# Queries of twelve of twenty-four groups loaded as eight-token runs and put in order by four copies out of PSUM

## The chip, the cores and the metric

The kernel runs on one core of one Trainium2 chip. The time is the device time of one execution in microseconds (us); the kernel before took 178.64 us as the median of three runs (177.48 to 182.0). Another execution was recorded by the hardware profiler; durations below come from that one.

The core has an engine for matrix products (PE; its weight loads are PEld), three engines for elementwise work (DVE, ACT, POOL), and SP, which here only issues DMAs. Sixteen DMA engines move the data. SBUF and PSUM are the on-chip memories, both with 128 partitions; matrix products land in PSUM.

## The reference

Four batches, eight heads, 768 tokens, head dimension 64, all fp32. A linear attention with a per-head decay `lam` comes first, then a layer that changes 128 chosen tokens of each batch:

```python
# attention, blocks of 64 tokens
intra = (q @ k.T * Dmask) @ v             # inside the block
inter = (q * lam_pow) @ kv_state          # from the blocks before
kv_state = lam_block * kv_state + (k * rev_pow).T @ v
# x: the heads side by side, 512 values for each token
scores = x @ w_gate
top    = the 128 highest scores of each batch
out[top] = x[top] + sigmoid(scores[top]) * (relu(x[top] @ w1) @ w2)
```

## The kernel before

A **group** is 128 tokens of one batch with all eight heads; there are 24 groups, numbered 0 to 23, six for each batch. For every group `load(g)` (L66 to L83) issues three DMAs from SP's queue: keys (`kn`), queries (`qn`) and values (`vn`), 256 KB each. In all three a partition holds one token: its row is eight pieces of 64 values, one for each head. In DRAM these pieces lie 768 tokens apart, so a piece, and a packet of the DMA, is 256 bytes, and a load has 1,024 packets.

`transposes(g, name)` (L192) turns the queries and the keys so that the head dimension lies over the partitions. For each pair of heads PE transposes a 128x128 block into a quarter of a PSUM bank (L203), and one ACT copy takes the whole bank into SBUF (L207). So `qT` has the two heads of a pair on partitions 0 to 63 and 64 to 127, and for each of the four pairs 128 tokens in order. POOL multiplies `qT` by the powers of the decay (`qs`, L216); PE reads `qT` for the scores (L240) and `qs` for the part from the states (L340).

The order of the work is written out by hand. The loop at L682 runs over g. For g of 11 and more (the second branch, L753) one pass is, on PE: the transposes of group g+1, queries first; one piece of the expert layer; `from_states(g)` (L340); `state_products(g+1)` (L287); the sums and the row for the ranking (L472, L434); two more pieces (L564 or L576); `from_scores(g)` (L363); `scores(g+1)` (L240). ACT follows in the same order: the copies of `qT` and `kT` (L207), then what the pieces and the ranking leave in PSUM (L540, L568, L437), then the three copies that make `x_b` (L391, L393). POOL runs `qs`, the decayed state (L300) and the decayed keys (L185). PSUM has four banks `m` that are handed out in turn.

SP takes its DMAs in order. At the start of pass g, `loads_to(g + ahead(g), g)` issues the loads of groups up to g + 4 (rising to 8 ahead), and after them some of the weights of the expert layer (`w_sb`, L97 and L102). At the end of the pass comes the store of finished groups (L398). The second branch first transposes group 12 in pass 11. Each group has its own buffers out of eight, and a DMA waits for the one eight before it on SP's queue.

Of the kernel before, what the change touches and what calls it, by code (L numbers as in the profile page):

```python
# [17 lines left out]
def kernel(  # L18
# [12 lines left out]
    nc = tc.nc  # L31
# [5 lines left out]
    L = 128  # L37
# [11 lines left out]
    WEIGHTS = {8: 1, 9: 2, 10: 1, 11: 3, 12: 3, 13: 2}  # L49
    WIDE = 11  # L50
    WARM = 8
    TINY = 2.0 ** -125
    BELOW = TINY * (1.0 - 2.0 ** -24)

# [7 lines left out]

    half = [slice(0, C), slice(C, 2 * C)]
    loaded = {}

    def load(g):  # L66
        b, c = divmod(g, NT)
        rows = slice(c * L, (c + 1) * L)
        srcs = (("kn", k), ("qn", q), ("vn", v))
        tiles = [ld.tile([128, H, D], FP32, name=name) for name, _ in srcs]  # L70
        whole, front, back = slice(0, H), slice(0, H // 2), slice(H // 2, H)
        order = [(x, whole) for x in range(3)]
        if g == 0:
            order = [(0, front), (1, front), (0, back), (1, back), (2, whole)]
        for x, hs in order:
            if (g, x) == (2, 2):
                nc.sync.dma_start(
                    out=wg_b[:], in_=moe_w_gate.unsqueeze(0).broadcast_to([128, HD])
                )
            nc.sync.dma_start(  # L80
                out=tiles[x][:, hs], in_=srcs[x][1][b, hs, rows, :].rearrange("h p d -> p h d")
            )
        loaded[g] = tiles  # L83
# [3 lines left out]
    wg_b = const.tile([128, HD], FP32, name="wg_b")  # L87
    wg_o = const.tile([128, HD], FP32, name="wg_o")
    load(0)
    load(1)  # L90
    load(2)
    w1_sb = const.tile([128, NDC, F], FP32, name="w1_sb")
    w2_sb = const.tile([128, NFC, HD], FP32, name="w2_sb")
# [18 lines left out]
    for hp in range(NHP):  # L112
        for hh in range(2):
            h = 2 * hp + hh
            nc.vector.tensor_tensor_scan(
                out=mask_w[:, hh, hp, :], data0=lam_b[:, h : h + 1].broadcast_to([128, L]),
# [35 lines left out]
    def warm(n):  # L152
        for _ in range(n):
            nc.tensor.matmul(
                free[-1][:, :L], lhsT=zero[:], rhs=zero[:], start=True, stop=True,
                skip_group_check=True,
            )

    warm(WARM)

    def bank(hold=False):
        t = next(t for t in free if not any(t is x for x in held))
        free[:] = [x for x in free if x is not t] + [t]
        if hold:
            held.append(t)
        return t

    qTs, qss, kTs, kds, ps_ = {}, {}, {}, {}, {}
# [23 lines left out]
    def transposes(g, name, part=None):  # L192
        if g >= NG:
            return
        t = loaded[g][1 if name == "qT" else 0]
        dsts = qTs if name == "qT" else kTs
        hps = range(NHP) if part is None else range(part * NHP // 2, (part + 1) * NHP // 2)
        if not part:
            banks_[name] = bank()
            dsts[g] = att.tile([128, NHP, L], FP32, name=name)  # L200
        tp = banks_[name]
        for hp in hps:
            nc.tensor.transpose(  # L203
                tp[:, hp * L : (hp + 1) * L], in_=t[:, 2 * hp : 2 * hp + 2, :], identity=ident[:]
            )
        at = slice(hps[0] * L, (hps[-1] + 1) * L)
        nc.scalar.copy(out=dsts[g][:].rearrange("p a i -> p (a i)")[:, at], in_=tp[:, at])  # L207

# [415 lines left out]
    def constants():  # L624
        nc.gpsimd.memset(lead[:], TINY)
        nc.gpsimd.affine_select(
            out=lead[:], in_=lead[:], compare_op=ALU.is_ge, fill=-BELOW,
            base=0, pattern=[[1, L]], channel_multiplier=-1,
        )
        nc.gpsimd.memset(ones[:], 1.0)  # L630
        nc.gpsimd.iota(slot_i[:], pattern=[[1, 128]], base=0, channel_multiplier=0)
        nc.gpsimd.iota(place_i[:, 0], pattern=[[1, NG]], base=0, channel_multiplier=0)
        nc.gpsimd.iota(place_i[:, 1], pattern=[[0, NG]], base=0, channel_multiplier=1)
# [48 lines left out]
    for g in range(-1, NG):  # L682
# [3 lines left out]
        if wide(g):  # L686
# [7 lines left out]
            if g < 0:  # L694
                for part in range(2):
                    transposes(0, "kT", part)
                    transposes(0, "qT", part)
# [4 lines left out]
            elif g == 0:  # L702
                transposes(1, "kT")
                from_scores(0, 0)
                transposes(1, "qT")
                from_scores(0, 1)
                outputs(0)
                store(0)
                queries_decayed(1)
                nc.scalar.copy(  # L710
                    out=decay_w[:], in_=qpow[:, :, L - 1 : L].broadcast_to([128, NHP, D])
                )
                decay_state(2)
            else:
                for name in ("kT", "qT") if g == 1 else ("qT", "kT"):
                    transposes(g + 1, name)
                queries_decayed(g + 1)
                from_scores(g)
                if g == 1:
                    nc.scalar.copy(  # L720
                        out=wg_o[:].rearrange("p (a b e) -> p a b e", a=2, e=D),
                        in_=wg_b[:].rearrange("p (b a e) -> p a b e", a=2, e=D),
                    )
                    gate_scores(0)
                outputs(g)
                store(g)
                gate_scores(g)
# [113 lines left out]
```

## Time and profile before

| what | value |
|---|---|
| time, median of 3 runs | 178.64 us (177.48 to 182.0) |
| time of the profiled execution | 179.35 us |
| its span | 177.6 us |
| PE busy | 161.5 us (91%) |
| DVE, ACT, POOL busy | 99.1, 68.9, 86.2 us |
| packets of the DMA queues | 82,608, of which 75,792 under 512 bytes |
| bytes moved | 32.20 MB |
| load of queries, 256 KB, issue to landing (median) | 5.1 us |
| TensorE clock, mean | 0.994 |

The span is what the profiler recorded from the first to the last instruction; the time of that execution is 1.75 us longer, and the execution is 0.71 us above the median of the three runs. The profile has the busy time of each engine, the same in 40 slices of the span, the DMA queues, a chain of waits followed back from the last instruction, the costliest groups of instructions, and the DMA issues. The trace behind it can be asked for windows of time and for single instructions, and holds a record of every DMA packet with its size and duration.

### The profile page before, as it was taken

How to read it: one execution, taken by the hardware profiler on the slowest of the kernel's cores; microseconds unless marked ns; L12 is line 12 of the kernel's file. 1: busy time of each engine (PE TensorE's matmuls, PEld its weight loads, DVE VectorE, ACT ScalarE, POOL GpSimd, SP SyncE). 2: the span in 40 equal slices, each digit the busy share in tenths (PEclk: the TensorE clock that was granted, in tenths of full speed). 3: DMA queues.
4: the chain of work that ended last, by engine and by line, in shares of the span. 5: the costliest groups of instructions: out<-in, count | busy, mean ns of one | idle time of the engine just before them, and what ended most of it. 6: DMA issues, size and time to landing. Idle time of an engine off the chain costs nothing.

```text
span 177.6 us, 7490 instructions
## 1 busy us (share of the span) xinstructions
PE 161.5 (91%) x3228; PEld 133.7 (75%) x3228; DVE 99.1 (56%) x304; ACT 68.9 (39%) x173; POOL 86.2 (49%) x96
## 2 busy tenths in 40 slices
PE   7998988999998999899695989999998999999990
PEld 7687966789887989897363679887665699559970
DVE  2876957678694748635627457647565767030011
ACT  3344436453343545434332364556244353013100
POOL 1396562546667656547374755827756300202022
PEclk9999999999999999999999999999999999999997
DMA  4999989999989999988989999999412131201000
GB/s 108 223 223 206 238 196 224 234 233 252 209 187 266 285 251 243 325 217 284 265 286 241 230 251 212 207 231 232 147 63 80 44 122 59 63 0 59 0 30 30
DMA packets 82608, 32.20 MB, mean 181 GB/s; under 512 B 75792, under 2 KB 77840, under 8 KB 82576
## 3 DMA queue, kind: packets, MB, share of 16 engines
q1 hardware_dynamic: 81776, 29.63, 70.3%
q0 software_dynamic: 656, 2.10, 3.9%
q8 instruction: 25, 0.41, 1.0%
q14 instruction: 7, 0.06, 0.1%
q10 hardware_dynamic: 144, 0.00, 0.0%
HBM read 24.38 MB, written 7.34 MB: 179 GB/s over the span
## 4 chain that ended last, share of the span: by engine, by line
PE 61%; DMA 18%; SPq 8%; issue 4%; ACT 3%; POOL 2%; DVE 2%; POOLq 1%; ACTq 0%
PE m L564 14%; PE m L576 11%; DMA qn<-in_q_dram 10%; PE m L203 9%; SPq L80 6%; PE o L356 4%; PE o L340 3%; DMA kn<-in_k_dram 3%; DMA wg_b<-in_moe_w_gate_dram 3%; PE o L363 3%; PE su L287 3%; PE su L240 3%; PE o L329 3%; PE su L234 2%; PE m L434 2%
## 5 line engine op out<-in xcount | busy, mean ns | idle before, releaser
L564 PE MATMUL m<-xsT,w_sb 128*128 128x128 f32 x256 | 31.3, 276 | 0.0
L564 PEld LDWEIGHTS m<-xsT,w_sb 128*128 128x128 f32 x256 | 30.0, 193 | 0.6 <-ACT xsT L540 0.6
L576 PE MATMUL m<-w_sb,hs 128*128 128x512 f32 (+1 forms) x80 | 30.1, 508 | 0.0
L216 POOL TENSOR_TENSOR qs<-qT,qpow 128x512 f32<-128x512 f32 x13 | 16.6, 1274 | 14.7 <-ACT qT L207 14.7
L300 POOL TENSOR_TENSOR decayed<-state,decay 128x256 f32<-128x256 f32 x21 | 16.5, 786 | 8.2 <-DVE ranks L476 6.2
L203 PE MATMUL m<-ident,qn 128*128 128x128 f32 x96 | 15.7, 283 | 5.1 <-DMA qn<-in_q_dram 4.6
L437 ACT COPY sc_row<-m 128x128 f32<-128x128 f32 x24 | 6.3, 266 | 32.6 <-PE m L434 23.5
L207 ACT COPY qT<-m 128x512 f32<-128x512 f32 (+1 forms) x25 | 14.2, 569 | 10.9 <-PE m L203 6.7
L576 PEld LDWEIGHTS m<-w_sb,hs 128*128 128x128 f32 x80 | 14.2, 193 | 5.6 <-issue 4.8
L185 POOL TENSOR_TENSOR kd<-kn,kpow 128x512 f32<-128x512 f32 x13 | 14.3, 1097 | 6.8 <-DMA kn<-in_k_dram 6.0
L185 POOL TENSOR_TENSOR kd<-kn,kpow_w 128x512 f32<-128x512 f32 x11 | 11.7, 1059 | 12.1 <-DMA kn<-in_k_dram 6.9
L207 ACT COPY kT<-m 128x512 f32<-128x512 f32 (+1 forms) x25 | 14.3, 574 | 6.0 <-PE m L203 6.0
L568 ACT ACTIVATE hs<-m 128x128 f32<-128x128 f32 x32 | 8.9, 279 | 17.9 <-PE m L564 17.9
L214 POOL TENSOR_TENSOR qs<-qT,qpow 128x512 f32<-128x512 f32 x9 | 11.5, 1274 | 8.8 <-ACT qT L207 8.6
L203 PEld LDWEIGHTS m<-ident,qn 128*128 128x128 f32 x96 | 10.3, 141 | 6.7 <-DMA qn<-in_q_dram 5.2
L203 PE MATMUL m<-ident,kn 128*128 128x128 f32 x96 | 14.8, 275 | 0.4 <-ACT kT L207 0.2
L319 DVE TENSOR_TENSOR state<-su,decayed 128x256 f32<-128x256 f32 x21 | 8.9, 424 | 9.9 <-POOL decayed L300 6.4
L254 DVE TENSOR_TENSOR p<-su,mask_w 128x1024 f32<-128x1024 f32 (+1 forms) x11 | 12.9, 1169 | 2.1 <-PE su L234 2.1
L356 PE MATMUL o<-vn,p 128*64 128x64 f32 x352 | 12.9, 225 | 0.2 <-DVE p L254 0.2
L356 PEld LDWEIGHTS o<-vn,p 128*64 128x64 f32 x352 | 11.3, 138 | 2.2 <-issue 1.4
L414 DVE CUSTOM_DVE_ANT_0 xg<-x_b,wg_b 128x512 f32<-128x512 f32 x14 | 11.4, 817 | 2.6 <-DMA wg_b<-in_moe_w_gate_dram 1.5
L407 DVE CUSTOM_DVE_ANT_0 xg<-o,wg_o 128x512 f32<-128x512 f32 x10 | 6.9, 690 | 10.2 <-ACT x_b L385 9.9
(86 smaller groups left out, 278.2 us busy)
## 6 DMA issues: line engine op xcount, KB each, us to landing
vn<-in_v_dram SPq DMA_DIRECT2D x24, 256.0 KB, 6.0
out_dram<-x_b SPq DMA_DIRECT2D x24, 256.0 KB, 4.7
kn<-in_k_dram SPq DMA_DIRECT2D x23, 256.0 KB, 5.1
qn<-in_q_dram SPq DMA_DIRECT2D x23, 256.0 KB, 5.1
w_sb<-in_moe_w_dram SPq DMA_DIRECT2D x4, 512.0 KB, 6.1
w_sb<-in_moe_w_dram SPq DMA_DIRECT2D x8, 256.0 KB, 4.8
kn<-in_k_dram SPq DMA_DIRECT2D x2, 128.0 KB, 3.3
qn<-in_q_dram SPq DMA_DIRECT2D x2, 128.0 KB, 3.4
```

The costliest lines, as they stand in the source:

```text
L80: nc.sync.dma_start(out=tiles[x][:, hs], in_=srcs[x][1][b, hs, rows, :].rearrange("h p d -> p h d"))
L185: nc.gpsimd.tensor_tensor(out=kd[:], in0=loaded[g][0][:], in1=pw[:].rearrange("p a b -> p (a b)").unsqueeze(2).broadcast_to([128, H, D]), ...
L203: nc.tensor.transpose(tp[:, hp * L : (hp + 1) * L], in_=t[:, 2 * hp : 2 * hp + 2, :], identity=ident[:])
L207: nc.scalar.copy(out=dsts[g][:].rearrange("p a i -> p (a i)")[:, at], in_=tp[:, at])
L214: nc.gpsimd.tensor_tensor(out=qs[:], in0=qTs[g][:], in1=qpow[:], op=ALU.mult)
L216: nc.gpsimd.tensor_tensor(out=qs[:].rearrange("p a (c i) -> p a c i", c=2), in0=qTs[g][:].rearrange("p a (c i) -> p a c i", c=2), in1=qpow ...
L254: nc.vector.tensor_tensor(out=ps_[g][:, :, at], in0=(o_ if part == 1 else su)[:, :, at], in1=mask_w[:].rearrange("p a b i -> p a (b i)")[: ...
L300: nc.gpsimd.tensor_tensor(out=t[:], in0=states[n][:], in1=(decay_w if wide(g) else decay)[:], op=ALU.mult)
L356: nc.tensor.matmul(o_[half[c], hh, hp * D : (hp + 1) * D], lhsT=p[:, hh, i0 : i0 + C], rhs=vn[:, 2 * hp + hh, :], start=(hp == 0 and g % N ...
L414: nc.vector.tensor_tensor_reduce(out=xg[:], in0=x_bs[b][:, t].rearrange("p a b e -> p (a b e)"), in1=wg_b[:], scale=1.0, scalar=0.0, op0=A ...
L564: nc.tensor.matmul(ph, lhsT=w1_sb[:, dc, f * 128 : (f + 1) * 128], rhs=keep["xsT"][:, dc, :], start=(dc == 0), stop=(dc == NDC - 1),)
L576: nc.tensor.matmul(py[:, e0:e1], lhsT=keep["hs"][:, f, :], rhs=w2_sb[:, f, e0:e1], start=(f == 0), stop=(f == NFC - 1),)
```

## The change

For groups 12 to 23 the queries are loaded in another layout. A partition now holds eight tokens in succession of one head, which are 2,048 bytes in succession in DRAM: partition 16h + o holds tokens 8o to 8o + 7 of head h. The load has 128 packets of 2 KB in place of 1,024 of 256 bytes, and the DMA's pattern on the DRAM side is eight heads, then sixteen runs, then 512 values; before it was 128 tokens, then eight heads, then 64 values.

PE's four transposes of a group keep their shape. Each now takes a pair of tokens of every run instead of a pair of heads, and its result has the two tokens of the pair on the two halves of the partitions and (head, run) along the row. Four ACT copies, each from 64 partitions to 64 and 256 values wide, put this in order: `fro` walks pieces of 16 values in PSUM, and `to` writes every value eight places (32 bytes) from the last. Two of the four copies go from one half of the partitions to the other. What `qT` holds afterwards is the same as before. Keys, values and groups 0 to 11 are as they were. No instruction changes its place in the order, and ACT has 36 more.

```diff
+    RUN = L // 16
+    def packed(g):
+        return g > WIDE
...
+            if x == 1 and packed(g):
+                nc.sync.dma_start(
+                    out=tiles[1][:].rearrange("p t d -> p (t d)"),
+                    in_=q[b, :, rows, :].rearrange("h (o t) d -> h o (t d)", t=RUN),
+                )
+                continue
             nc.sync.dma_start(
                 out=tiles[x][:, hs], in_=srcs[x][1][b, hs, rows, :].rearrange("h p d -> p h d")
             )
...
+        if name == "qT" and packed(g):
+            to = qTs[g][:].rearrange("p b (o j r) -> p r b j o", j=RUN // 2, r=2)
+            fro = tp[:].rearrange("p (j b a o) -> p a b j o", j=RUN // 2, a=2, o=16)
+            for r, hh in ((0, 0), (1, 1), (1, 0), (0, 1)):
+                nc.scalar.copy(out=to[half[hh], r], in_=fro[half[r], hh])
+            return
         at = slice(hps[0] * L, (hps[-1] + 1) * L)
         nc.scalar.copy(out=dsts[g][:].rearrange("p a i -> p (a i)")[:, at], in_=tp[:, at])
```

## The prediction

> **What bounds the kernel.** I read the slices first: which engine is full, and when.
>
> ```profile
> PE   7998988999998999899695989999998999999990
> ACT  3344436453343545434332364556244353013100
> DMA  4999989999989999988989999999412131201000
> DMA packets 82608, 32.20 MB, mean 181 GB/s; under 512 B 75792, under 2 KB 77840, under 8 KB 82576
> q1 hardware_dynamic: 81776, 29.63, 70.3%
> PE 61%; DMA 18%; SPq 8%; issue 4%; ACT 3%; POOL 2%; DVE 2%; POOLq 1%; ACTq 0%
> ```
>
> The sixteen DMA engines are full until about 124 us (28 slices of 4.44 us), and nearly all their packets are small. PE is almost full too, with dents in slices 20 and 22. The chain of waits puts 18% on DMA. The windows say which of the two ends last, and where (columns: busy time and count of PE, PEld, DVE, ACT, POOL, then the clock, the DMA engines' share, GB/s):
>
> ```profile
> 60.00:72.00 12.00, 11.80 (x294) 10.93 (x291) 7.23 (x25) 5.95 (x16) 8.01 (x9) 1.00 1.09 260
> 72.00:98.00 26.00, 21.46 (x536) 16.28 (x535) 14.46 (x45) 9.59 (x27) 14.02 (x14) 1.00 0.99 270
> 98.00:122.00 24.00, 22.91 (x580) 19.88 (x582) 13.96 (x49) 11.34 (x31) 14.75 (x16) 1.00 0.99 228
> 122.00:141.00 19.00, 18.55 (x453) 12.32 (x446) 11.68 (x38) 7.76 (x20) 10.64 (x11) 1.00 0.36 105
> ```
>
> From 72 to 98 us PE is idle for 4.5 us while the DMA engines stand at 0.99. Before and after that PE is busy for 95% and more. PE's timeline names what it waits for: the transposes of the queries of groups 15, 16 and 17, and then no longer group 18 (start, duration, in brackets the idle time):
>
> ```profile
> 81.06 0.66 PE L203 MATMUL m<-ident,qn 128*128 128x128 f32 x4 [0.26 <-DMA qn<-in_q_dram]
> 89.03 0.66 PE L203 MATMUL m<-ident,qn 128*128 128x128 f32 x4 [1.86 <-DMA qn<-in_q_dram]
> 97.23 0.65 PE L203 MATMUL m<-ident,qn 128*128 128x128 f32 x4 [1.92 <-DMA qn<-in_q_dram]
> 102.46 0.66 PE L203 MATMUL m<-ident,qn 128*128 128x128 f32 x4
> ```
>
> So the queries set the pace up to 97.23 us, and PE from there to the end. What the change does to the DMA engines' work ahead of the landing at 97.2 us is what moves the end. Counting SP's query loads back from the last (120.16 us, group 23), group 12 is issued at 53.39 and group 17 at 91.34: **six** changed loads lie before that landing, all in a stretch with full engines. The other six come after it. Group 18's, issued at 95.71, lands at about 100.8 with the median of 5.1 us, 1.6 us before its use, and the slack grows to some ten us for group 23 (issued 120.16, used 135.67).
>
> **The load, as DMA work.** The packet records of the trace give 73,728 packets of 256 B, median 18 ns, mean 19.9, and 4,224 of 2 KB, median 84 ns, mean 96.7. (With 2,048 of 1 KB at 51.5 ns that is 1,978 us of engine time, 69.6% of sixteen times 177.6 us, so the records account for the 70.3% above.) Today a query load gives each engine 64 packets: 64 x 19.9 = 1.27 us. Afterwards it has 128 packets, and what they cost depends on two things that no row shows.
>
> The first is **over how many engines they go**. Every load in this trace has a pattern whose outermost dimension has 128 steps; the new one's outermost DRAM dimension has 8 (heads). If it is still dealt out to sixteen engines, each has 8 packets: 8 x 84 to 8 x 106.5 = 0.67 to 0.85 us, a gain of 0.42 to 0.60 us a load. If it is dealt out by its eight outer steps, eight engines have 16 packets each and the other eight none: 16 x 84 = 1.34 us at the least. I take eight, because eight steps are what the pattern offers, and keep sixteen as a rival. [...]
>
> The second is **the packet's time on those eight**. The eight also carry their full share of keys, values, weights and stores, so what counts is the load's time on them, not the mean of all sixteen. Bounds from 2-KB rows: 84 ns (median) and 151 ns (95th percentile). Nearest are single 256-KB stores with loads around them. The four of 97 to 120 us have means of 85.8, 121.0, 109.2 and 109.9 ns, together 106.5. Then 16 x 106.5 = 1.70 us, which is 0.43 us more than 1.27. From the ends: 16 x 84 - 1.27 = +0.07, 16 x 151 - 1.27 = +1.15. Six loads before the last DMA-set wait: **6 x 0.43 = +2.6 us** (+0.4 to +6.9). The six after it add as much to the DMA stream but nothing to the end: group 18 is 7 x 0.43 = 3.0 us later, where PE comes 2.6 us later and there were 1.6 us of slack; at the upper end 8.05 against 6.9 + 1.6 still fits.
>
> **The issue.** It stays one DMA in the same place on SP's queue, with nothing moved past it. SP takes 0.50 to 2.98 us for a query load, mostly held back by queues that are full, and the load lands 5 us after its issue, so there are several DMAs of cover: even if each of the new pattern took the longest issue in place of the shortest (+2.5 us), that is half the cover. Nothing; with the cover gone it would be up to 2.5 us a load.
>
> **The four copies.** The row nearest is L393, 64 partitions by 256 values out of PSUM, two in a row and partly across the halves: 366 ns, 0.74 for two. Four are 4 x 0.366 = 1.47 us where one copy took 0.586: +0.88 us. Writing every 32 bytes has no row; below I see no gain, above I take the whole-bank copy's 0.586 for each, 2.34 us, +1.76. I take 0.88. Twelve groups: ACT 68.9 + 10.6 = 79.5 us of the span.
>
> What waits for them? Behind them on ACT stand the `kT` copy, `xsT` and the relus. POOL's `qs` waits for `qT` already (14.7 us over 11 waits). Its next instruction, L300, then idles 0.92 to 1.25 us in most passes for a state that DVE makes, which covers 0.88. PE needs `qT` and `kT` only in `scores`, some 5 us after the transposes. The closest cover is `xsT` in pass 17: copied until 104.84, read by PE at 106.05, so 1.21 us. That holds 0.88, and at 1.76 it would cost 0.55. Pass 11 has the same pattern (63.40, read at 64.29: 0.89), ahead of the DMA waits that swallow it. I count +0.1, the cover being thin; 0 to +0.55.
>
> PE's instructions, the states, the stores and the weights do not change: nothing.
>
> **Sum.** +2.6 + 0.1 = +2.7 us on the profiled execution's 179.35 = 182.05 us. That execution is 0.71 above the median; on the median it is 178.64 + 2.7 = **181.3 us**, +1.5%. About 2% (3.6 us) is what a measurement of this kernel can tell from no change.
>
> **Rivals.**
>
> *All sixteen engines carry it.* For it: smaller total work, 0.42 to 0.60 us a load. Against: the eight outer steps. Six loads give -2.5 to -3.6 us, within the 4.0 us of waits that are there to lose; 175.0 to 176.2, and only at its very end over 2% faster.
>
> *Engines get in each other's way.* The new load gives an engine sixteen neighbouring partitions in place of its usual ones, and the eight idle engines run ahead into the next load meanwhile. If writes meet in SBUF, a packet costs up to the 151 ns that one in twenty costs now: +1.15 a load, +6.9 us, 185.5. For it: 2-KB transfers among loads already go up to 121 ns. Against: the median stays at 84. It decides from +0.6 a load, 117 ns a packet: slower than 2%. [...]
>
> *The load is hidden anyway*: the other streams reach PE as late, and the queries' own time does not show. 178.6, within 1. Against it: three waits that name `qn`.
>
> **Chances.** Forecast (84 to 117 ns on eight engines) 0.38; sixteen engines 0.16; collisions 0.38; hidden 0.08. Slower by over 2%: the collisions and a little of the forecast's upper end, 0.42. Faster by over 2%: part of the sixteen, 0.07. Within 2%: the rest, 0.51. The range takes in sixteen engines at its middle (175.8) and the collisions with a copy's worst (178.64 + 6.9 + 0.55 = 186.1). The forecast's own range is 179.0 to 182.6.
>
> **What would show it.** 81,776 packets on q1 become 71,024 in any case, and ACT gets 36 instructions and about 10.6 us. Eight engines: the DMA share between 72 and 98 us falls clearly under 0.99 while PE's waits at the query transposes grow from 4.0 to about 6.6 us. Sixteen: the share stays and the waits shrink to about 1. Collisions: 2-KB packets with a median over 117 ns. I am wrong on ACT if a copy takes over 0.5 us or PE waits for `xsT` or `kT`; wrong altogether if the landing of group 17's queries moves and the end does not.

## The result and the profile after

The changed kernel takes 185.81 us (median of four runs, 185.34 to 186.22) against 178.77 us for the kernel before, measured beside it (median of four runs): a ratio of 1.042, 95% interval 1.035 to 1.049, about 7 us slower. In two later sessions the same kernel came out at 1.025 (1.019 to 1.031) and 1.041 (1.034 to 1.049). The direction was as forecast and the time lies at the upper end of the range; the size, +2.7 us forecast, does not fit. The ratios leave out runs over 1.5% above the fastest of the same kernel, which are up to three quarters of a kernel's runs, so a median of all runs and a ratio can differ by a per cent; the profiles of e7, e8, e9, e10 and e12 are of such slower runs.

The profiled execution took 185.34 us, its span is 183.6 us (6.0 more than before). The page after, with the slices, the packets, the largest queue and the engines' shares of the chain of waits:

```profile
PE   7998998999999688988859969799989999999990
ACT  3344474444444648757464794685684755113100
DMA  5999899999999999999998978995110331101000
DMA packets 71760, 32.20 MB, mean 175 GB/s; under 512 B 63408, under 2 KB 65456, under 8 KB 71728
q1 hardware_dynamic: 70928, 29.63, 68.2%
PE 51%; ACT 16%; issue 12%; DVE 5%; SPq 5%; POOL 5%; DMA 4%; POOLq 1%; ACTq 0%
```

The packets fell as foreseen. Of those of 4 bytes, sixteen for each of the 111 DMAs of this queue before (1,776), 1,680 are left: eight fewer for each of the twelve new loads. But DMA, 18% of the chain before, is 4% now, ACT, 3% before, is 16%, and "issue", 4% before, is 12% (the last section says what a part of it is). ACT's slices from the fourteenth to the thirty-fourth are at 4 to 9 tenths where they were at 2 to 6. The costliest groups say with what (busy time, mean of one; then the idle time of the engine before them):

```profile
L232 POOL TENSOR_TENSOR qs<-qT,qpow 128x512 f32<-128x512 f32 x13 | 16.5, 1267 | 37.9 <-ACT qT L220 37.3
L220 ACT COPY qT<-m 64x256 f32<-64x256 f32 x48 | 29.8, 621 | 3.1 <-PE m L213 2.4
```

Each of the 48 new copies takes **621 ns**, not 366. POOL's wait for `qT` rose from 14.7 to 37.3 us. PE's timeline has the query load only once among its waits, and ACT in its place (L220 are the new copies, L223 the copy of `kT`, L450 the row for the ranking, L580 two pieces of the expert layer, L556 the copy of `xsT`). First the largest sums of the waits named after ACT (us in total, times, longest), then rows of the timeline:

```profile
PE m L450 <- ACT qT L220: 2.7, 6, 0.7
PE m L580 <- ACT xsT L556: 1.6, 2, 0.8
PE m L580 <- ACT kT L223: 1.1, 4, 0.3
```

```profile
68.24 0.66 PE L213 MATMUL m<-ident,qn 128*128 128x128 f32 x4 [0.32 <-DMA qn<-in_q_dram]
71.84 0.32 PE L450 MATMUL m<-ident,sc 128*128 128x128 f32 x1 [0.35 <-ACT qT L220]
72.45 2.05 PE L580 MATMUL m<-xsT,w_sb 128*128 128x128 f32 x16 [0.29 <-ACT kT L223]
79.54 2.05 PE L580 MATMUL m<-xsT,w_sb 128*128 128x128 f32 x16 [0.29 <-ACT kT L223]
89.94 0.52 PE L379 MATMUL o<-vn,p 64*64 64x64 f32 x20 [0.71 <-issue]
96.14 0.33 PE L303 MATMUL su<-vn,kd 64*64 64x64 f32 x3 [2.20 <-issue]
```

With two smaller ones PE's waits for the copies of `qT`, `kT` and `xsT` sum to 5.9 us; before they were 0.2.

Windows of the same stretches as before (PE, PEld, DVE, ACT, POOL, clock, DMA share, GB/s):

```profile
60.00:72.00 12.00, 9.63 (x229) 8.58 (x229) 6.23 (x22) 8.15 (x18) 4.46 (x6) 1.00 1.01 244
72.00:98.00 26.00, 21.44 (x475) 16.38 (x475) 11.94 (x37) 15.15 (x35) 13.67 (x15) 1.00 0.98 268
98.00:122.00 24.00, 21.36 (x516) 17.64 (x515) 14.87 (x50) 16.69 (x39) 13.11 (x14) 1.00 0.95 225
122.00:141.00 19.00, 17.76 (x442) 12.65 (x444) 10.03 (x35) 12.14 (x27) 11.32 (x12) 1.00 0.30 81
```

PE now stands idle for a part of every stretch, also after 98 us, where it had been the bound itself. The passes can be measured from one group's first query transpose to the next's. From group 12's to group 17's it is 36.13 us before and 39.25 after; from group 17's to group 23's, where before PE alone set the pace, 38.44 and 41.59; from there to the end 41.9 and 42.3. That is +3.1, +3.2 and +0.4, less 0.7 us that the profile after has gained ahead of group 12. The first of these is not clear of chance: e4 below, which differs from the kernel before only by loads after the last store, has 39.55 us there.

### The profile page after: what moved, and what is told of

It reads as the page before. It is cut to its first block, busy times and chain, and to the rows that moved or that the text cites. A ratio compares the mean times of both kernels' runs of the same rounds, so it can differ in the third digit from the quotient of the medians.

```text
span 183.6 us, 7526 instructions
## 1 busy us (share of the span) xinstructions
PE 163.7 (89%) x3228; PEld 134.5 (73%) x3228; DVE 97.8 (53%) x304; ACT 91.6 (50%) x209; POOL 85.8 (47%) x96
## 3 DMA queue, kind: packets, MB, share of 16 engines
q1 hardware_dynamic: 70928, 29.63, 68.2%
## 4 chain that ended last, share of the span: by engine, by line
PE 51%; ACT 16%; issue 12%; DVE 5%; SPq 5%; POOL 5%; DMA 4%; POOLq 1%; ACTq 0%
PE m L580 12%; PE m L592 10%; ACT qT L220 10%; PE m L213 6%; PE o L372 4%; SPq L90 4%; PE su L250 4%; PE o L379 3%; DMA vn<-in_v_dram 3%; PE o L345 3%; PE su L256 2%; PE m L450 2%; ACT kT L223 2%; ACT x_b L409 2%; PE m L294 2%
## 5 line engine op out<-in xcount | busy, mean ns | idle before, releaser
L580 PE MATMUL m<-xsT,w_sb 128*128 128x128 f32 x256 | 31.9, 278 | 2.7 <-ACT xsT L556 1.6
L232 POOL TENSOR_TENSOR qs<-qT,qpow 128x512 f32<-128x512 f32 x13 | 16.5, 1267 | 37.9 <-ACT qT L220 37.3
L580 PEld LDWEIGHTS m<-xsT,w_sb 128*128 128x128 f32 x256 | 29.8, 192 | 4.5 <-ACT xsT L556 2.6
L220 ACT COPY qT<-m 64x256 f32<-64x256 f32 x48 | 29.8, 621 | 3.1 <-PE m L213 2.4
L592 PE MATMUL m<-w_sb,hs 128*128 128x512 f32 (+1 forms) x80 | 30.1, 508 | 0.0
L592 PEld LDWEIGHTS m<-w_sb,hs 128*128 128x128 f32 x80 | 14.3, 194 | 5.6 <-issue 4.8
L316 POOL TENSOR_TENSOR decayed<-state,decay 128x256 f32<-128x256 f32 x21 | 17.2, 821 | 1.6 <-DVE ranks L492 1.5
L223 ACT COPY kT<-m 128x512 f32<-128x512 f32 (+1 forms) x25 | 14.3, 571 | 6.4 <-PE m L213 6.1
L213 PE MATMUL m<-ident,kn 128*128 128x128 f32 x96 | 15.3, 281 | 0.1
L195 POOL TENSOR_TENSOR kd<-kn,kpow 128x512 f32<-128x512 f32 x13 | 13.5, 1042 | 0.7 <-DMA kn<-in_k_dram 0.7
L379 PEld LDWEIGHTS o<-vn,p 64*64 64x64 f32 x416 | 7.6, 134 | 7.3 <-issue 4.2
L250 PE MATMUL su<-qT,kT 64*128 64x128 f32 x168 | 12.3, 285 | 0.1
```

Source lines behind the costliest of these rows:

```text
L195: nc.gpsimd.tensor_tensor(out=kd[:], in0=loaded[g][0][:], in1=pw[:].rearrange("p a b -> p (a b)").unsqueeze(2).broadcast_to([128, H, D]), ...
L213: nc.tensor.transpose(tp[:, hp * L : (hp + 1) * L], in_=t[:, 2 * hp : 2 * hp + 2, :], identity=ident[:])
L220: nc.scalar.copy(out=to[half[hh], r], in_=fro[half[r], hh])
L232: nc.gpsimd.tensor_tensor(out=qs[:].rearrange("p a (c i) -> p a c i", c=2), in0=qTs[g][:].rearrange("p a (c i) -> p a c i", c=2), in1=qpow ...
L250: nc.tensor.matmul(to[:, hh, hp * L : (hp + 1) * L], lhsT=kT[half[hh], hp, :], rhs=qT[half[hh], hp, :], start=True, stop=True, skip_group_ ...
L316: nc.gpsimd.tensor_tensor(out=t[:], in0=states[n][:], in1=(decay_w if wide(g) else decay)[:], op=ALU.mult)
```

## The experiments

Theory A, formed on this profile: the slow copies make the loss, because they hold ACT and the PSUM banks that PE wants next. Theory B is the prediction's: the load on eight engines makes it.

**The load alone, and the copies alone.** e1 keeps the load and drops the sorting; e2 keeps the old load and makes after's four copies.

```diff
 e1_load_only
-        if name == "qT" and packed(g):
-            ... (the four copies)
 e2_copies_only
-            if x == 1 and packed(g):
-                ... (the 2-KB load)
```

> The new load stays, the four copies are replaced by the one whole-bank copy of before, so the queries of groups 12 to 23 stay unsorted (the reordering is left out). Theory A (the copies cost the 7 us, by holding ACT and the PSUM banks): back to 176 to 179 us, no PE wait named after an ACT copy of qT. Theory B (the load costs it, on eight engines with slow packets): 183 to 186 us, and PE's waits on the query loads of groups 15 to 17 grow from 4.0 us to 8 or more.

> The load of before, and the four copies of after on its transposes (they sort what needs no sorting, so the queries of groups 12 to 23 are out of order). Theory A: 184 to 188 us, with copies of about 620 ns each. Theory B: 178.5 to 180 us, since the load is as before.

Measured: e1 1.013 (1.007 to 1.019), e2 1.014 (1.003 to 1.026). Neither theory had that: together the two parts came to less than the whole in its first session, and each was small. By the medians of the same runs that the ratios use, e1 is 0.6% over before (180.75 against 179.72 us) and e2 2.6% (184.32), so both ratios are uncertain by about a per cent. PE's waits on the query loads did not grow in e1 (2.2 us in all against 4.6 before); e2's copies took 621 ns and PE waited for them as in after. The two parts were timed in another session than after, so the sum was left open.

**Eight engines or sixteen.** e3 is e1 with the runs outermost in the DRAM pattern, e4 has six lone loads at the quiet end of the kernel before.

```diff
-                    in_=q[b, :, rows, :].rearrange("h (o t) d -> h o (t d)", t=RUN),
+                    in_=q[b, :, rows, :].rearrange("h (o t) d -> o h (t d)", t=RUN),
```

> As e1_load_only, but with the sixteen runs outermost in the DRAM pattern in place of the eight heads: the same 128 packets of 2 KB, and sixteen outer steps. The reordering is left out. If the outer steps set how many engines carry a load, this one has sixteen: 2-KB packets nearer to 84 ns than e1's, and a time 1 to 4 us under e1. If they do not, the same time as e1 within 0.5 us.

> The kernel before with six more loads of 256 KB of queries into a tile of their own, one after the other, in the quiet stretch after the last store: the old pattern, heads outermost, runs outermost, and all three again. By packet records: the old one 64 packets of 18 ns an engine, 1.15 us from the first packet to the last; heads outermost on eight engines 16 x 84 = 1.34 us, on sixteen 0.67 us; runs outermost 0.67 us.

e3: 0.992 (0.989 to 0.996), 2.1% under e1. e4, from the packet records of single loads (span from the first packet's start to the last one's end; the sum of the packets' times over the span is the number of engines at work; the first of the old pattern ran into a store and is left out):

| pattern | packets | span us | engines at work |
|---|---|---|---|
| old, tokens outermost | 1,024 of 256 B | 1.31 | 13.9 |
| heads outermost | 128 of 2 KB | 2.12, 1.69 | 6.4, 7.0 |
| runs outermost | 128 of 2 KB | 1.33, 1.41 | 11.7, 10.3 |

So the new load does go over **eight engines** (6.4 and 7.0 at work on the mean, and eight packets of 4 bytes a load where the old has sixteen), and lone it takes 0.4 to 0.8 us longer than the old one. SP took 641 and 768 ns to issue it, and 398 and 431 ns for the old pattern. With the runs outermost it goes over more than eight (11.7 and 10.3 at work; that it is all sixteen is the author's estimate from its sixteen outer steps), and that did not bring the expected 0.67 us: 16 and 13 of its packets took over 200 ns, the longest 654 and 625 (with the heads outermost 9 and 3, the longest 639 and 313).

**What makes a copy slow.** e5 has the old load and the copies in four forms, three groups each.

```diff
+            ... (five views of qT and PSUM)
+            for r, hh in order:
+                if g < 15:    # runs of 64 read, runs of 64 written
+                    nc.scalar.copy(out=plain[half[hh], r], in_=src[half[r], hh])
+                elif g < 18:  # pieces of 16 read, written in a row
+                    nc.scalar.copy(out=piece[half[hh], r], in_=fro[half[r], hh])
+                elif g < 21:  # j innermost: read 512 bytes apart, written 8 apart
+                    nc.scalar.copy(
+                        out=sorted_[half[hh], r].rearrange("p b j o -> p b o j"),
+                        in_=fro[half[r], hh].rearrange("p b j o -> p b o j"),
+                    )
+                else:         # as after: o innermost, written 32 bytes apart
+                    nc.scalar.copy(out=sorted_[half[hh], r], in_=fro[half[r], hh])
```

> The load of before, and four copies of 64 partitions by 256 values in four forms (the queries of groups 12 to 23 end up out of order): groups 12 to 14 runs of 64 read and written; 15 to 17 read in pieces of 16 as after, written in a row; 18 to 20 read every 512 bytes, written every 32 bytes in the other loop order; 21 to 23 as after. If the 32-byte step of the writes costs the time, the first two forms take about 370 ns and the last two about 620. If the pieces of 16 in the reads cost it, the second form takes 620 as well. If it is the crossing of the halves, all forms are slow.

The copies of `qT` in e5 (duration in ns: least, median, most), in the order of the four forms:

```profile
L219 ACT COPY qT<-m x12: 364/368/370, 62.0 to 77.1; 64x256 f32<-64x256 f32 x12
L221 ACT COPY qT<-m x12: 364/366/369, 83.0 to 99.2; 64x256 f32<-64x256 f32 x12
L223 ACT COPY qT<-m x12: 377/388/399, 103.4 to 118.5; 64x256 f32<-64x256 f32 x12
L228 ACT COPY qT<-m x12: 611/620/630, 123.7 to 140.3; 64x256 f32<-64x256 f32 x12
```

The expectation had the third form wrong: with the loops turned round its innermost write step is 8 bytes, and 32 only in the loop outside. Neither the halves nor the pieces read from PSUM cost anything (368 and 366 ns); the same 256 places written in the other order cost 388 ns in place of 620. What is slow is an **innermost write step of 32 bytes** on ACT.

**Do four fast copies cost?** e7 has the old load and four copies of plain runs.

```diff
+            to = qTs[g][:].rearrange("p b (r x) -> p r b x", r=2)
+            fro = tp[:].rearrange("p (b a x) -> p a b x", b=NHP, a=2)
+            ... (the loop of four copies, as in after)
```

> The load of before, and four copies of the same size that read and write runs of 64 (the queries of groups 12 to 23 end up out of order): some 370 ns each, the +0.88 us a pass that the prediction counted in place of the +1.9 us of after. The prediction's step (0.88 us is covered): a ratio of 0.997 to 1.003. If any lengthening of the copies is paid for, in proportion: about half of e2_copies_only's 1.4%, 1.007.

366 ns each and 0.989 (0.978 to 1.000, by two runs of e7): no loss. The prediction's cover for +0.88 us a pass held in the time, though PE waits 1.0 us for `xsT` and 0.4 us for `kT` in e7's profile.

**After with the runs outermost and the slow copies**: e6 has e3's pattern, and PSUM is read accordingly.

```diff
+            fro = tp[:].rearrange("p (j o b a) -> p a b j o", j=RUN // 2, a=2, o=16)
```

> After with the sixteen runs outermost in the load's DRAM pattern; PSUM is then read every 32 bytes, and the queries come out in order. If the two costs of after are separate (eight engines, and copies that hold ACT), only the copies are left: a ratio of 1.00 to 1.02 to before, like e2_copies_only less the 0.8% of e3_load_runs_outer. If the copies alone with the smaller packets cost the 4%, 1.035 to 1.05.

1.031 (1.022 to 1.040): with the load on more than eight engines nearly all of the loss is still there. That speaks against B, and against e2's 1.014.

**After with the loops turned round.** e9 has the heads outermost, e10 the runs, e11 the runs for all groups but the first; e8 is after itself beside them.

```diff
-            to = qTs[g][:].rearrange("p b (o j r) -> p r b j o", j=RUN // 2, r=2)
-            fro = tp[:].rearrange("p (j b a o) -> p a b j o", j=RUN // 2, a=2, o=16)
+            to = qTs[g][:].rearrange("p b (o j r) -> p r b o j", j=RUN // 2, r=2)
+            fro = tp[:].rearrange("p (j b a o) -> p a b o j", j=RUN // 2, a=2, o=16)
 e10, e11: the load of e3, and
+            fro = tp[:].rearrange("p (j o b a) -> p a b o j", j=RUN // 2, a=2, o=16)
 e11:
+        return g > 0
```

> After, unchanged, beside the next three: a ratio of 1.03 to 1.05 to before. Its profile is a second look at the PE waits of 0.96, 0.71 and 2.20 us that the first put down to issue between the transposes of groups 15 and 18. If the load on eight engines makes them, 2 to 4 us again in that stretch; if they were chance, under 1 us.

> After with the loops of the four copies in the other order, so that the innermost step of the writes is 8 bytes in place of 32; the queries come out in order. Copies of about 390 ns. If the 621-ns copies made the larger part of the loss, what is left is the load's: 1.005 to 1.02, as e1_load_only. If the number of copies (four in place of one) made it, 1.03 or more.

> As e9_heads_swapped, with the sixteen runs outermost in the load's pattern. Both costs gone: as e3_load_runs_outer, 0.985 to 1.0. If it is over 1.01, the four copies of 390 ns cost PE something after all.

> As e10_runs_swapped, for all groups but the first. The DMA engines are as full in the first 57 us, so if they set the pace there too, 1 to 4 us under e10; if the other engines do, the same as e10 or up to 2 us over it, for ACT has 0.9 us more in each of these passes.

e8 1.025 (1.019 to 1.031); e9 **1.000** (0.994 to 1.006); e10 0.998 (0.993 to 1.004); e11 1.011 (1.002 to 1.020). Copies of 389 ns take the whole loss away with the load left as it is. e10 beats neither before nor e9 clearly. In e11 the stretch from group 12 to 17 is the shortest of all profiles (33.45 us), but group 12 is reached at 64.84 us, where the profiles of the kernels that are alike up to there have 60.35 to 63.99. That four copies of 390 ns are not free in the first half is the likely reason, but not shown.

**The parts beside the whole on one chip.**

> e1_load_only once more (the reordering is left out), beside the other parts on one chip. If the eight-engine load costs by itself, 1.005 to 1.02 again, and over e14 by at least 0.005; if e9_heads_swapped's 0.9998 is the truth, 0.99 to 1.005.

> e2_copies_only once more (the queries of groups 12 to 23 end up out of order). If the slow copies make nearly all of after's loss, 1.02 to 1.035, the same as e15_after_third; if half of it, 1.01 to 1.018.

> e3_load_runs_outer once more (the reordering is left out): 0.985 to 1.0. PE's waits put down to issue between the transposes of groups 12 and 17: under 1 us, against 2 to 4 us for e12 and e15 if loads on eight engines delay PE's instructions.

> After once more, unchanged, beside its parts on the same chip: a ratio of 1.025 to 1.045 to before, the span of its two sessions so far.

e12 0.999 (0.992 to 1.005, by three of twelve runs; the median of all twelve is 1.1% over that of all of before's), e13 **1.042** (1.034 to 1.050), e14 0.996 (0.991 to 1.000), e15 **1.041** (1.034 to 1.049). The copies alone cost as much as the whole change, and PE waits 6.1 us in e13 for the copies of `qT`, `kT` and `xsT`, as in after (5.9). e2's 1.014 was low, by three runs. Theory A stands; of B there remains a cost of the load alone between nothing (e12, e9) and 1.3% (e1), which these runs don't settle.

The stage times agree. From group 17's transposes to group 23's the six profiles with slow copies have 41.5 to 42.9 us, the ten others 37.4 to 40.0 (e5, with its mixed forms, is left out).

**How the copies set the pace.** Four rows of ACT's timeline of after, and two of PE's, from one pass:

```profile
120.16 0.37 ACT L407 COPY x_b<-o 128x256 f32<-128x256 f32 x1 [0.38 <-PE o L379]
120.54 0.75 ACT L409 COPY x_b<-o 64x256 f32<-64x256 f32 x2
121.32 2.53 ACT L220 COPY qT<-m 64x256 f32<-64x256 f32 x4
123.87 0.59 ACT L223 COPY kT<-m 128x512 f32<-128x512 f32 x1
```

```profile
117.42 2.05 PE L580 MATMUL m<-xsT,w_sb 128*128 128x128 f32 x16 [0.29 <-ACT kT L223]
119.40 0.69 PE L379 MATMUL o<-vn,p 64*64 64x64 f32 x32
```

They close a ring: PE's pieces and `from_scores` (117.42 to 120.16, 2.74 us), the three `x_b` copies (1.16), the four of `qT` (2.55), that of `kT` and the handing over of its bank (0.64 to 124.51), and PE's pieces again, for which that bank had to come free (the 0.29 us that PE waits for L223). 2.74 + 1.16 + 2.55 + 0.64 = 7.09 us. After has it twice, 72.45 to 79.54 and 117.42 to 124.51; e2, e6, e13 and e15 have passes of 7.08 to 7.10 at the same places. Before, the one `qT` copy takes 0.49 from start to start, so the ring is 5.03 us long, and a pass with no other wait takes PE 6.26: a cover of 1.23 us. The slow copies add 2.06, and the 0.83 over the cover is paid in such a pass (7.09 - 6.26). The pass from group 21 to 22, with the larger pieces (L592), goes from 6.04 to 6.61. The other passes are longer by other waits as well; in them the longest waits for ACT are those of the ranking row for the bank that the `qT` copies hold (up to 0.7 us) and of the pieces for `xsT` (0.8).

## Why the prediction was right or wrong

**Direction and range** held, but by luck: 2.6 of the 2.7 us forecast stood for the load, and the range's upper end for collisions of its packets, and neither made the loss. The size failed, 2.7 against some 7 us (4.5 to 7.5 by the three sessions).

**The step that failed is "The four copies"**: it put +0.1 us on the end for them, and alone they measured 1.042 (e13), some 7.4 us. The cover was about right: 1.21 us by `xsT`, and 1.23 by the ring. With copies of 366 and 389 ns e7 and e9 lose nothing. The term that was mis-sized is the copy itself: 621 ns, 2.55 for four, +2.06 a pass. That is beyond the upper end of +1.76, because "the whole-bank copy's 0.586 for each" was no bound: a 128x512 copy writes more values, but in a row, and took 586 ns where these took 621. And "What waits for them?" was answered by what reads the copies' results; it left out that PE also waits for the PSUM banks that the copies of `qT` and `kT` hold (the ranking row 2.7 us, the pieces 1.1; neither reads `qT` or `kT`). So at the upper end one `xsT` wait of 0.55 was counted, where pass after pass pays.

**The load**, +2.6, was right in its form and is not shown in its size. It goes over eight engines, as taken (6.4 and 7.0 at work in e4). Its packets took longer than the 106.5 ns: all 2-KB packets sum to 615.1 us after and 408.5 before, which leaves 134 ns for each of the 1,536 new ones, if the others cost what they did; the loads of groups 12 and 13, whose packets stand apart in the records, have means of 138 and 134 ns. That is over the 117 ns from which the collisions rival was to decide, and 16 x 134 = 2.15 us a load would have given 6 x 0.88 = +5.3 us. Yet e12 and e9 put the load at nothing and e1 at +1.3%. So **"six loads before the last DMA-set wait"** did not reach the end in the way that was forecast: PE's waits for the queries did not grow, they fell from 4.6 us to 2.2 in e1 and to 0.3 in e12.

**The rivals.** *Sixteen engines*: not this kernel; spread over more engines by hand (e3, e14; 10.3 and 11.7 at work in e4) the load gains 0.4 to 0.8%, 0.8 to 1.4 us, not 2.5 to 3.6, and the interval of e14 (0.991 to 1.000) just reaches no gain. *Collisions*: its packet price came where the new packets stand apart (median 128 ns in both loads of after; 85 over all its 2-KB packets), its loss did not. Nor do the eight engines make that price: in e3, with the runs outermost, the same two loads have means of 134 and 151 ns. *Hidden anyway*: given 0.08, it is the nearest to what e9 and e12 show of the load.

**What was to show it.** The packets (70,928 against 71,024) and the 36 instructions came. The DMA share from 72 to 98 us did not fall (0.98): all packet records together sum to 2,144 us after and 2,143 before. ACT rose by 22.7 us, not 10.6. "Wrong on ACT if a copy takes over 0.5 us or PE waits for `xsT` or `kT`": all three, 0.62, and waits of 1.6 and 1.1 us.

**What the packets and the copies show.** In e4 6.4 and 7.0 engines were at work with eight steps outermost, 10.3 and more with sixteen, and the twelve loads left eight packets of 4 bytes fewer each.

A copy of 512 values took 586 ns and one of 256 took 366, which is 0.86 ns for each further value; 8 bytes apart the 256 took 388, and 32 bytes apart 620. No run had a step between the two, so where the price begins is not shown. As an estimate from e5, the 32-byte step costs (620 - 388) / 256 = 0.9 ns a value over the 8-byte one.

## What to carry to other kernels

When a copy puts values in order, try the loops both ways round: on ACT the same 64x256 copy took 388 ns with its writes 8 bytes and its reads 512 bytes apart, and 620 with its writes 32 bytes apart and its reads in pieces of 16 in a row. Price a new access pattern by a run of that pattern; a larger copy with runs was no upper bound for it (586 ns against 621). And where an engine looks half idle, follow the ring (copy, bank, matrix product, next copy) and compare its length with the pass: 1.2 us of cover here, and past it PE waits.

## What the runs showed of the hardware that was not expected

**PE waits at fixed places in its program, for packets of instructions.** PE's waits that the profile puts down to issue stand in the middle of a batch of matrix products, in all kernels at the same instruction (the 27th of L379's 32, in the next pass the tenth, in the one after it the 30th of L303's). e9's windows between four such places (PE and PEld with their counts):

```profile
75.79:82.61 6.82, 5.57 (x126) 5.12 (x126) 3.62 (x10) 3.14 (x9) 4.03 (x4) 1.00 0.97 266
82.61:89.11 6.50, 6.07 (x126) 3.80 (x126) 3.08 (x11) 3.52 (x9) 2.66 (x4) 1.00 0.99 295
89.11:94.86 5.75, 4.08 (x127) 3.06 (x127) 1.54 (x4) 3.24 (x8) 2.62 (x3) 1.00 1.03 289
```

There are 252 to 254 of PE's instructions from one to the next, and the trace has an instruction queue with 25 packets of 16,384 bytes for PE's 6,456, one for 258. That these waits are for the next packet of instructions is borne out by the times of these packets. Between 58 and 100 us the seventeen profiles together have 34 waits of 0.2 us and more that are put down to issue, and 33 of them stand at six such places. In each of the 33 a packet of that queue had ended 1.1 to 1.8 us before PE went on; at the 52 passages where it had ended more than 1.8 us before, PE did not wait.

These waits sum to 3.9, 3.9, 1.8, 3.4, 5.2 and 1.2 us in after, e1, e8, e9, e12 and e15, which have the load on eight engines, and to 0 to 1.5 us (mean 0.6) in the eleven others, e3 and e14 with their 2-KB packets and the runs outermost among them (0 and 0.7). So PE's instructions tend to come later beside loads on eight engines; the two sets overlap (without e7, e8, e9, e10 and e12 it is 3.9, 3.9 and 1.2 against 0 to 1.0 us), and why was not tried. In e1 and e12 these waits, not the queries, are where PE stands longest. They are not what after loses: e13 has none of them there and is as slow.
